# Convolution-kernel rows copied from tile to tile instead of through DRAM, and PSUM copies of the last block shared by two engines

## The chip, the core and the metric

One core of a Trainium2 chip runs the whole program. The metric is the device time of one launch in microseconds (us), from start to end of the program on that core. Five engines work beside each other, each through its own list of instructions in a fixed order: TensorE (PE in the profile; its weight loads are PEld), VectorE (DVE), ScalarE (ACT), GpSimd (POOL) and SyncE (SP). SP, ACT and POOL also issue DMA transfers; in the profile these issues are SPq, ACTq and POOLq.

## The reference

The reference computes one layer and all its gradients. With `x` of 2048 rows and 512 columns:

```
xn = layernorm(x)
K  = real(sum over n of C * exp(dt*A*l) * dt*B)      # 512 channels, l = 0..2047, 128 states
s  = irfft(rfft(xn, 4096) * rfft(K, 4096))[:2048] + xn * Dskip     # along the 2048 rows
g  = silu( silu(xn @ w1) @ w2 )                      # w1: 512 x 1792, w2: 1792 x 512
out = x + s * g
```

Its outputs are `out` and the gradients of `x`, of the seven arrays behind `K`, of `Dskip`, `w1` and `w2` for a given gradient of `out` (the gradient of an unused input is not among the work). Everything is bf16 outside; sums are made in fp32.

## The kernel before, in words

The 512 channels are worked in four blocks (b = 0 to 3) of 128. The long convolution is done as a Fourier transform written as matmuls. For each block in the forward part there are three generators, which the program weaves together:

- `gen_tables(b)` makes the convolution kernel K of the block. In two halves it builds powers of exp(dt*A) on DVE and ACT (`V`, `sn`, `E`, `YD`, `H`, lines 434 to 459), multiplies them into weight tiles `W` (line 468, DVE), and PE sums over the states into PSUM tiles `ps_k` (line 473), which ACT copies to `Xr`. At the end PE regroups `Xr` into two PSUM tiles `ps_e` (line 484), and ACT copies these in 12 pieces to the tile `KE` (lines 491 to 506). `KE` takes turns with `W` in one pool entry with two buffers (tag "W"). Its rows then go to the DRAM array `Kd` by four DMAs issued by ACT (line 508).
- `gen_conv_x(b)` transforms the block's columns of `xn`.
- `gen_conv_fwd(b)` loads `Kd` into the tile `Kb` by one DMA issued by SP (lines 531, 532), transforms it (`dft_fwd`, lines 289 to 318), multiplies by the transform of `xn` on DVE (`cplx_mul`, lines 341 to 355), transforms back (`dft_inv`, lines 321 to 338) and adds the skip term on DVE into `S_b` (lines 544, 545). `dft_fwd` and `dft_inv` hand 12 PSUM tiles of 128 x 1024 per call chain to an evacuation helper `ev`: four `dA` after line 299, four `dA` after line 315, four `dB` after line 328. In before, this helper is `k.evc`, which always uses ACT (line 45). The two transposed tiles `pt_f` between them always go to DVE (line 46). The PSUM tiles of the transforms come from a pool with two buffers ("pc"); those of the dense layers and transposes from one with three ("pf").

Beside these runs the dense forward part (`gen_ffn_fwd`): eight chunks of 256 rows, each with 56 matmuls at line 567 (PSUM to `hT` by ACT), two silu activations to `aT` at line 575, and 28 matmuls at line 585 (PSUM to `ob` or `YD` by ACT). When its last chunk is under way, `W1` is turned in place (seven PSUM tiles of transposes at line 112, copied back by ACT and DVE in turn). After block 3's tables, `gen_conv_fwd(3)`, the last chunk and two gate loops run together: line 613 (silu, ACT), 615 (DVE), 628 (derivative of silu, ACT), 629 and 631 (DVE). The first gate loop's silu and the second's derivative need different activation tables, so a change from one to the other costs an ACT_TABLE_LOAD. Then `last` columns are multiplied (line 1165, DVE), `W2` is turned, and the backward part begins, whose first dense matmuls are those at line 926.

The order of the Python text isn't the order on the engines. The framework plans each engine's list when the program is built, from its own estimates of when things will be ready, and within a pool entry it picks the buffer that its plan frees first. A change of a few lines therefore reorders instructions far around it. Each engine then works strictly in its planned order. Transfers issued by SP and ACT are counted on eight semaphores in turn; a transfer waits, before it is issued, for the last earlier one on its semaphore to land.

Of the kernel before, what the change touches and what calls it, by code (L numbers as in the profile page):

```python
# [13 lines left out]
BF16 = mybir.dt.bfloat16  # L14
# [4 lines left out]
P = 128  # L19
# [109 lines left out]
def run(gen):  # L129
    for _ in gen:  # L130
        pass
# [157 lines left out]
def dft_fwd(k, w8, U, ev):  # L289

    nc, pc = k.nc, k.pc
    A = w8.tile([P, 2, 16, P], BF16, name="dA", tag="w8")
    Av = A[:].rearrange("p c g k -> p (c g k)").rearrange("p (g c t e) -> p c g t e", c=2, t=16, e=4)
    B = w8.tile([P, 2, 16, P], BF16, name="dB", tag="w8")
    for c in range(2):
        for h in range(2):
            ps = pc.tile([P, 8, P], F32, name="ps_s1", tag="pc")
            for j in range(8):
                nc.tensor.matmul(out=ps[:, j], lhsT=k.TF[:, 8 * h + j, c, :], rhs=U(8 * h + j), start=True, stop=True)  # L299
            ev(Av[:, c, :, 8 * h:8 * h + 8, :], ps[:].rearrange("p t (g e) -> p g t e", e=4))  # L300
    yield
    for u in range(2):
        pt = pc.tile([P, 16, P], BF16, name="pt_f", tag="pc")
        for j in range(16):
            nc.tensor.transpose(out=pt[:, j], in_=A[:, u, j, :], identity=k.ident[:])
        k.evq(B[:, u], pt[:])
    for _ in range(LAG - 1):
        yield
    Bv = B[:].rearrange("p u (g h) k -> p u h g k", h=2)
    for u in range(2):  # L310
        for c in range(2):
            ps = pc.tile([P, 8, P], F32, name="ps_s2", tag="pc")
            for v in range(2):
                for h in range(2):
                    nc.tensor.matmul(out=ps[64 * h:64 * h + 64, 4 * v:4 * v + 4], lhsT=k.F2[:, c, :], rhs=Bv[:, u, h, 4 * v:4 * v + 4, :],  # L315
                                     start=True, stop=True)
            ev(A[:, c, 8 * u:8 * u + 8, :], ps[:])
    return A, B


def dft_inv(k, A2, Y, ev, consume):

    nc, pc = k.nc, k.pc
    for g0 in range(0, 16, 4):
        ps = pc.tile([P, 4, 32, 8], F32, name="ps_i2", tag="pc")
        for g in range(4):
            for c in range(2):
                nc.tensor.matmul(out=ps[:, g], lhsT=Y[:, c, g0 + g, :], rhs=k.I2[:, c].rearrange("p c m -> p (c m)"),  # L328
                                 start=(c == 0), stop=(c == 1))
        ev(A2[:].rearrange("p c t (g e) -> p g (c t) e", e=8)[:, g0:g0 + 4], ps[:])  # L330
    yield
    for h in range(2):
        ps = pc.tile([P, 8, P], F32, name="ps_i1", tag="pc")
        for j in range(8):
            t = 8 * h + j
            for c in range(2):
                nc.tensor.matmul(out=ps[:, j], lhsT=k.TI[:, 2 * t + c, :], rhs=A2[:, c, t, :], start=(c == 0), stop=(c == 1))
        consume(8 * h, 8, ps)


def cplx_mul(k, w8, a, b, conj=False):

    TT = k.nc.vector.tensor_tensor
    n = 8
    for g0 in range(0, 16, n):
        gs = slice(g0, g0 + n)
        t2 = w8.tile([P, 2, n, P], BF16, name="cm2", tag="cm2")
        TT(out=t2[:, 0], in0=b[:, 1, gs], in1=a[:, 1, gs], op=ALU.mult)
        TT(out=t2[:, 1], in0=b[:, 0, gs], in1=a[:, 1, gs], op=ALU.mult)
        TT(out=b[:, :, gs], in0=b[:, :, gs], in1=a[:, 0:1, gs].to_broadcast([P, 2, n, P]), op=ALU.mult)  # L350
        TT(out=b[:, 0, gs], in0=b[:, 0, gs], in1=t2[:, 0], op=ALU.add if conj else ALU.subtract)  # L351
        if conj:
            TT(out=b[:, 1, gs], in0=t2[:, 1], in1=b[:, 1, gs], op=ALU.subtract)
        else:
            TT(out=b[:, 1, gs], in0=b[:, 1, gs], in1=t2[:, 1], op=ALU.add)
# [61 lines left out]
def gen_tables(k, b):  # L417

    nc, tbl = k.nc, k.tbl
# [66 lines left out]
    KE = tbl.tile([P, 8, 8, 32], BF16, name="KE", tag="W", bufs=2)  # L486
    bc = lambda ap, n: ap.unsqueeze(2).to_broadcast([P, ap.shape[1], n, 32])
    ev = k.evk
# [15 lines left out]
    ev(KE[:, 2:8, 6:8, :], bc(B[:, 6:12], 2))  # L504
    ev(KE[:, 4:8, 5, :], B[:, 8:12])
    ev(KE[:, 4:8, 4, :], B[:, 12:16])
    for a in range(4):
        nc.scalar.dma_start(k.Kd[b, a].rearrange("i j r -> j i r"), KE[a:P:4].rearrange("p i t q -> p i (t q)"))
    yield


def spectrum_in(k, w8, b, which):
    t = w8.tile([P, 2, 16, P], BF16, name="sp_in", tag="w8")
    k.nc.sync.dma_start(t[:].rearrange("p c g k -> p (c g k)"), {"U": k.Ud, "K": k.KXd}[which][b])
    return t
# [11 lines left out]
def gen_conv_fwd(k, b):  # L527

    nc, dft = k.nc, k.dft
    bs = slice(b * P, b * P + P)  # L530
    Kb = dft.tile([P, 4, 16, 32], BF16, name="Kb", tag="t4")
    nc.sync.dma_start(Kb[:].rearrange("p a t q -> p a (t q)"), k.Kd[b].rearrange("a i (r s) x -> (i r) a (s x)", s=2))
    for _ in range(LAG):
        yield
    KX, A2 = yield from dft_fwd(k, dft, lambda t: Kb[:, :, t, :], k.evc)
    U = spectrum_in(k, dft, b, "U")
    nc.sync.dma_start(k.KXd[b], KX[:].rearrange("p c g k -> p (c g k)"))
    yield
    cplx_mul(k, dft, KX, U)
    S = dft.tile([P, 16, P], BF16, name="S_b", tag="t4")  # L540

    def consume(t0, n, ps):
        xd = dft.tile([P, 8, P], BF16, name="xd", tag="cm2")
        nc.vector.tensor_tensor(out=xd[:], in0=k.xn[:, t0:t0 + n, bs], in1=k.Dbc[:, bs].unsqueeze(1).to_broadcast([P, n, P]), op=ALU.mult)
        nc.vector.tensor_tensor(out=S[:, t0:t0 + n], in0=ps[:], in1=xd[:], op=ALU.add)
    yield from dft_inv(k, A2, U, k.evc, consume)
    k.S_b = S
    (nc.scalar if b == 3 else nc.sync).dma_start(k.Sd[b], S[:].rearrange("p t d -> p (t d)"))
    yield
# [496 lines left out]
def kernel(ctx, tc, A_u, A_A_re, A_A_im, A_B_re, A_B_im, A_C_re, A_C_im, A_log_dt, A_Dskip, B_x, B_w1, B_w2, grad_out,  # L1046
           out_0, out_1, out_2, out_3, out_4, out_5, out_6, out_7, out_8, out_9, out_10, out_11):
    nc = tc.nc
    k = KCtx()
# [10 lines left out]
    def pool(name, side=None, es=ctx, **kw):  # L1060
        kw.setdefault("bufs", 1)
        return es.enter_context(tc.tile_pool(name=name, side=side, reuse_waits="tile", **kw))
    dr = ctx.enter_context(tc.tile_pool(name="dram", bufs=1, space=DRAM))
    NB = 4
# [7 lines left out]
    k.dUd = dr.tile([NB, P, L], BF16, name="dUd")  # L1072
    k.Ud = dr.tile([NB, P, 4096], BF16, name="Ud")
    k.KXd = dr.tile([NB, P, 4096], BF16, name="KXd")
    k.Kd = dr.tile([NB, 4, 8, 32, 256], BF16, name="Kd")
    k.dKd = dr.tile([NB, 4, 8, 32, 256], BF16, name="dKd")
    k.Ed = dr.tile([NB, 2, P, 2 * 16 * NE * 4], BF16, name="Ed")
    k.Yd = dr.tile([NB, 2, P, 2 * 16 * P], BF16, name="Yd")
# [11 lines left out]
    es_f, es_x, es_t = (ctx.enter_context(ExitStack()) for _ in range(3))  # L1090
# [1 line left out]
    wt = pool("wt", es=es_d)  # L1092
    k.W1 = wt.tile([P, k.DK, F], BF16, name="W1")
    k.W2 = wt.tile([P, k.FT, D], BF16, name="W2")
    k.p1 = pool("p1", es=es_f)
    k.fp = pool("fp", es=es_f)
    with ExitStack() as es_s:
        wp = pool("setup", side="right", es=es_s)
        ldt = wp.tile([P, D], BF16, name="ldt")
        nc.scalar.dma_start(ldt[:], A_log_dt.unsqueeze(0).to_broadcast([P, D]))  # L1100
        nc.scalar.dma_start(k.Dbc[:], A_Dskip.unsqueeze(0).to_broadcast([P, D]))
        xl = load_x(k, wp)
        x_sb = next(xl)
        S = load_params(k, wp, 0, D, ("Ar", "Ai"))
        next(xl)
        nc.sync.dma_start(k.W1[:], B_w1.rearrange("(k p) f -> p k f", p=P))
        next(xl); next(xl)
        S.update(load_params(k, wp, 0, D, ("Br", "Bi", "Cr", "Ci")))
        nc.sync.dma_start(k.W2[:], B_w2.rearrange("(k p) d -> p k d", p=P))
        consts = make_consts(k, wp)  # L1110
        k.ident = k.const.tile([P, P], BF16, name="ident")
        nc.gpsimd.memset(k.ident[:], 0.0)
        nc.gpsimd.affine_select(out=k.ident[:], in_=k.ident[:], compare_op=ALU.not_equal, fill=1.0,
                                base=0, pattern=[[-1, P]], channel_multiplier=1)
        k.zero = k.const.tile([P, P], BF16, name="zero")
        nc.gpsimd.memset(k.zero[:], 0.0)
        k.onesf = k.const.tile([P, 1], F32, name="onesf")
        nc.gpsimd.memset(k.onesf[:], 1.0)
        k.ecst = k.const.tile([P, NE + len(Y_EXP)], F32, name="ecst")
        for i, e in enumerate(E_EXP + Y_EXP):  # L1120
            nc.gpsimd.memset(k.ecst[:, i:i + 1], float(e))
        ssm_magnitudes(k, wp, S, ldt[:])
        next(consts)
        ln = layer_norm(k, wp, x_sb)
        next(ln)
        k.XT = [turned_rows(k, k.fp, k.xn, c, "XT", k.evx) for c in range(2)]
        next(ln)
        next(consts)
        next(ln)
        ssm_weights(k, wp, S)  # L1130
        next(ln)
        run(consts)
# [83 lines left out]
```

## Time and profile before

| | |
|---|---|
| median of 3 runs | 691.67 us (687.14 to 695.03) |
| the profiled execution: its own time | 689.59 us |
| its span in the profile | 687.8 us |
| mean granted TensorE clock | 0.968 |
| PE busy | 594.7 us (86% of the span) |
| DVE busy | 505.9 us (74%) |
| ACT busy | 466.7 us (68%) |
| POOL busy | 81.7 us (12%) |
| `Kd` writes | 16 DMAs of 128 KB, issued by ACT |
| `Kb` loads | 4 DMAs of 512 KB, issued by SP |

Times in the text are microseconds from the start of the span. "Busy" counts compute instructions; the time in which ACT or SP issues a transfer is not in it. In a row of the timeline the first number is the start, the second the length, and in brackets stands how long the engine was idle before and what ended that. Some matmul records can be missing, and matmul ends are modelled.

### The profile page before, as it was taken

Reading aid. Unit: us, or ns where it says so; the run is one execution under the profiler, and the core shown is the slowest. Engines: PE = TensorE matmul, PEld = TensorE weight load, DVE = VectorE, ACT = ScalarE, POOL = GpSimd, SP = SyncE. Lnnn points to the kernel's source line nnn. Section 1 sums busy time; section 2 is a strip of 40 time slices with the busy share of each in tenths; the row PEclk is TensorE's granted clock in tenths of the full one; section 3 lists DMA queues with packets and bytes.
Section 4 is the critical chain, followed back from the end, with each engine's and each line's share of the span. In section 5 each row is a group of like instructions: output and inputs, shape, how many; then the busy total and the mean of one; then the engine's idle time right before and its main releaser. Section 6 shows DMA issues by size and latency. Waiting matters only on the chain. (4 is left out here: it accounts for less than half of the span.)

```text
span 687.8 us, 14419 instructions
## 1 busy us (share of the span) xinstructions
PE 594.7 (86%) x5884; PEld 434.3 (63%) x5884; DVE 505.9 (74%) x904; ACT 466.7 (68%) x628; POOL 81.7 (12%) x164
## 2 busy tenths in 40 slices
PE   0587987999999996689797999978998998999988
PEld 0455755676676664466575676747676765755877
DVE  6979998768968956979785969537688864756950
ACT  6878768889879888996656586335638764635531
POOL 2354100100101100000000000000002020123210
PEclk9988998999999999799999999999999999999999
DMA  9965455745746969777826755579979999238994
GB/s 286 341 152 210 179 202 193 274 165 215 278 138 239 325 234 314 240 252 242 274 77 217 219 187 192 150 175 219 258 151 287 209 221 229 89 115 273 228 285 103
DMA packets 158690, 148.54 MB, mean 216 GB/s; under 512 B 79264, under 2 KB 136096, under 8 KB 155040
## 3 DMA queue, kind: packets, MB, share of 16 engines
q1 hardware_dynamic: 145664, 125.07, 64.2%
q0 software_dynamic: 6064, 17.57, 6.8%
q10 hardware_dynamic: 6896, 4.98, 2.3%
q8 instruction: 46, 0.75, 0.5%
q14 instruction: 20, 0.16, 0.1%
HBM read 65.14 MB, written 64.10 MB: 188 GB/s over the span
## 5 line engine op out<-in xcount | busy, mean ns | idle before, releaser
L45 ACT CAST dA<-ps_s 128x1024 bf16<-128x1024 f32 x96 | 93.4, 1024 | 10.6 <-PE ps_s L299 6.8
L773 DVE TENSOR_TENSOR Tp<-Vb,Eb 128x1344 bf16<-128x1344 bf16 x64 | 51.8, 851 | 20.7 <-ACT Vb L45 11.8
L926 PE MATMUL ps_da<-doT,W 128*128 128x256 bf16 x448 | 60.9, 277 | 4.2 <-DVE dhT L928 2.6
L45 ACT CAST dB<-ps_i 128x1024 bf16<-128x1024 f32 x48 | 47.0, 1024 | 25.7 <-PE ps_i L328 18.9
L567 PE MATMUL ps_h<-XT,W 128*128 128x256 bf16 x448 | 63.0, 281 | 1.5 <-ACT hT L45 0.8
L928 DVE TENSOR_TENSOR dhT<-ps_da,dhT 128x512 bf16<-128x512 f32 x56 | 37.9, 686 | 35.5 <-PE ps_da L926 25.5
L328 PE MATMUL ps_i<-I,sp_in 128*128 128x256 bf16 x384 | 52.8, 286 | 8.9 <-DVE sp_in L351 6.4
L585 PE MATMUL ps_o<-W,aT 128*128 128x512 bf16 x224 | 55.2, 385 | 1.1 <-ACT aT L575 0.9
L937 PE MATMUL ps_dx<-W,dhT 128*128 128x512 bf16 x224 | 54.8, 379 | 0.4 <-DVE dhT L928 0.4
L567 PEld LDWEIGHTS <-W 128*128 128x128 bf16 x448 | 42.2, 100 | 16.3 <-issue 9.6
L328 PEld LDWEIGHTS <-sp_in 128*128 128x128 bf16 x384 | 37.5, 102 | 23.7 <-DVE sp_in L351 10.5
L926 PEld LDWEIGHTS <-W 128*128 128x128 bf16 x448 | 42.2, 99 | 15.8 <-issue 10.4
L969 PE MATMUL ps_w<-YD,a_tok 128*128 128x512 bf16 x224 | 51.5, 379 | 0.0
L987 PE MATMUL ps_w<-dh_tok,xn 128*128 128x256 bf16 x448 | 49.5, 272 | 2.3 <-DMA dh_tok<-DHd 2.3
L45 ACT CAST Vb<-ps_v 128x672 bf16<-128x672 f32 x64 | 42.3, 725 | 12.9 <-PE ps_v L763 12.9
L45 ACT CAST o<-ps_w 128x256 bf16<-128x256 f32 (+1 forms) x42 | 18.0, 439 | 48.5 <-PE ps_w L987 20.7
L987 PEld LDWEIGHTS <-xn 128*128 128x128 bf16 x448 | 43.6, 98 | 8.2 <-issue 3.0
L473 PE MATMUL ps_k<-W,YD 128*128 128x84 bf16 x512 | 29.7, 210 | 11.5 <-DVE W L468 6.7
L315 PE MATMUL ps_s<-dB,F 128*64 128x512 bf16 x192 | 32.5, 390 | 6.8 <-ACT dB L45 2.3
L473 PEld LDWEIGHTS <-YD 128*128 128x128 bf16 x512 | 25.4, 104 | 19.3 <-issue 13.8
L299 PEld LDWEIGHTS <-TF 128*128 128x128 bf16 x384 | 26.1, 101 | 18.0 <-issue 10.8
L585 PEld LDWEIGHTS <-aT 128*128 128x128 bf16 x224 | 21.1, 99 | 25.5 <-issue 3.9
(226 smaller groups left out, 1267.4 us busy)
## 6 DMA issues: line engine op xcount, KB each, us to landing
Yd<-YD SPq DMA_DIRECT2D x8, 1024.0 KB, 4.3
sp_in<-Ud SPq DMA_DIRECT2D x8, 1024.0 KB, 7.5
h_in<-Hd SPq DMA_DIRECT2D x14, 512.0 KB, 4.4
Ed<-E SPq DMA_DIRECT2D x8, 672.0 KB, 4.0
Eb<-Ed SPq DMA_DIRECT2D x8, 672.0 KB, 5.3
Hd<-hT POOLq DMA_DIRECT2D x8, 512.0 KB, 6.3
Ud<-dA SPq DMA_DIRECT2D x4, 1024.0 KB, 6.0
KXd<-dA SPq DMA_DIRECT2D x4, 1024.0 KB, 5.2
```

What stands on the lines that cost most here:

```text
L45: return self.nc.scalar.copy(out=out, in_=in_)
L315: nc.tensor.matmul(out=ps[64 * h:64 * h + 64, 4 * v:4 * v + 4], lhsT=k.F2[:, c, :], rhs=Bv[:, u, h, 4 * v:4 * v + 4, :], start=True, stop= ...
L328: nc.tensor.matmul(out=ps[:, g], lhsT=Y[:, c, g0 + g, :], rhs=k.I2[:, c].rearrange("p c m -> p (c m)"), start=(c == 0), stop=(c == 1))
L473: nc.tensor.matmul(out=ps[:, q], lhsT=Y[:, m % 2, q0 + 4 * u + q].rearrange("p j a -> p (j a)"), rhs=W[:, m, 4 * u + q].rearrange("p e a - ...
L567: nc.tensor.matmul(out=ps[:, j], lhsT=k.W1[:, dk, ft * P:ft * P + P], rhs=XTv[:, :, dk, :], start=(dk == 0), stop=(dk == DK - 1))
L585: nc.tensor.matmul(out=ps[:], lhsT=aT[:, ft, t * P:t * P + P], rhs=k.W2[:, ft, :], start=(ft == 0), stop=(ft == FT - 1))
L773: k.nc.vector.tensor_tensor(out=Tp[:, c, :, r ^ c].rearrange("p e (q w) a -> p q w e a", w=2), in0=Vb[:, :, c].rearrange("p q w (e a) -> p ...
L926: nc.tensor.matmul(out=ps[:, j], lhsT=k.W2[:, ft, dk * P:dk * P + P], rhs=dTv[:, :, dk, :], start=(dk == 0), stop=(dk == DK - 1))
L928: nc.vector.tensor_tensor(out=dh[:, i0:i0 + 2, :], in0=ps[:], in1=dh[:, i0:i0 + 2, :], op=ALU.mult)
L937: nc.tensor.matmul(out=ps[:], lhsT=dhs[ft // 8][:, ft % 8, t * P:t * P + P], rhs=k.W1[:, :, ft * P:ft * P + P], start=(ft == 0), stop=(ft ...
L969: nc.tensor.matmul(out=ps[:], lhsT=at[:, t, :], rhs=k.do[:, t, :], start=(t == 0), stop=(t == k.T - 1))
L987: nc.tensor.matmul(out=ps[:], lhsT=k.xn[:, t, dk * P:dk * P + P], rhs=dh[:, t].rearrange("p j n -> p (j n)"), start=(t == 0), stop=(t == k ...
```

## The change

`Kb` is now written directly from `KE`, by eight DMAs from tile to tile issued by SP (one for each group of 16 destination partitions) at the end of `gen_tables`; `Kd` in DRAM, its four writes and its load are gone. `Kb` has another order of its inner dimensions, and `dft_fwd` reads it accordingly; each DMA carries 128 rows of 512 bytes. `Kb` is allocated when the tables are made and handed on through `k.Kb`. For block 3 alone, the 12 PSUM copies of `gen_conv_fwd` go to ACT and DVE in turn. The pool `p1` (masks and small constants of the tables) is opened after `fp` and closed with the tables.

```
-    for a in range(4):
-        nc.scalar.dma_start(k.Kd[b, a].rearrange("i j r -> j i r"), KE[a:P:4].rearrange("p i t q -> p i (t q)"))
+    k.Kb[b] = k.dft.tile([P, 2, 4, 8, 32], BF16, name="Kb", tag="t4")
+    for i in range(8):
+        nc.sync.dma_start(k.Kb[b][16 * i:16 * i + 16].rearrange("r s a t q -> r (s a) (t q)"), KE[:, i].rearrange("p t q -> p (t q)"))
     yield
...
 def gen_conv_fwd(k, b):
     nc, dft = k.nc, k.dft
+    ev = Evac(nc, "AD") if b == 3 else k.evc
     bs = slice(b * P, b * P + P)
-    Kb = dft.tile([P, 4, 16, 32], BF16, name="Kb", tag="t4")
-    nc.sync.dma_start(Kb[:].rearrange("p a t q -> p a (t q)"), k.Kd[b].rearrange("a i (r s) x -> (i r) a (s x)", s=2))
+    Kb = k.Kb.pop(b)
     for _ in range(LAG):
         yield
-    KX, A2 = yield from dft_fwd(k, dft, lambda t: Kb[:, :, t, :], k.evc)
+    KX, A2 = yield from dft_fwd(k, dft, lambda t: Kb[:, t // 8, :, t % 8, :], ev)
...
-    yield from dft_inv(k, A2, U, k.evc, consume)
+    yield from dft_inv(k, A2, U, ev, consume)
...
-    k.Kd = dr.tile([NB, 4, 8, 32, 256], BF16, name="Kd")
+    k.Kb = {}
...
-    k.p1 = pool("p1", es=es_f)
     k.fp = pool("fp", es=es_f)
+    k.p1 = pool("p1", es=es_t)
```

## The prediction, made before the changed kernel had run

> **What bounds the kernel now.** I read the page's busy table first (PE 86%, no engine full), then a table of stages. The two programs list the same matmuls, and from the 2425th on (the first at line 926) all engines' orders agree, so the time of that matmul decides. It starts at 298.48. The stages are cut at the end of block 0's `KE` copies, at the first matmul on `Kb`, at the end of block 3's regrouping, and there. Columns: stretch, its length, then busy time of PE, PEld, DVE, ACT, POOL, granted clock, DMA share, GB/s.
>
> ```profile
> 99.18:111.66 12.48, 6.25 (x77) 4.92 (x78) 9.27 (x17) 6.63 (x9) 0.57 (x1) 0.73 0.58 197
> 111.66:245.50 133.84, 130.70 (x1390) 91.70 (x1389) 109.70 (x152) 117.75 (x170) 10.87 (x14) 1.00 0.65 235
> 245.50:298.48 52.98, 37.43 (x379) 27.84 (x377) 37.68 (x54) 47.99 (x52) 0.00 (x0) 0.85 0.78 250
> 298.48:687.80 389.32, 354.20 (x3463) 264.00 (x3461) 264.39 (x506) 218.48 (x292) 37.77 (x68) 0.99 0.78 203
> ```
>
> The long second stage is PE's (98%). In the third ACT is fullest (48.0 of 53.0) and PE waits. The first is a hole: PE is busy for half of it, at a clock of 0.73. The timeline says why:
>
> ```profile
> 99.18 4.78 ACTq L508 DMA_DIRECT2D Kd<-KE  x4
> ...
> 104.00 0.44 ACT L45 CAST Xr<-ps_k 128x336 bf16<-128x336 f32 x1 [4.36 <-issue]
> ...
> 104.50 0.97 PE L473 MATMUL ps_k<-W,YD 128*128 128x84 bf16 x16 [2.94 <-ACT Xr L45]
> ...
> 107.31 1.63 DVE L468 TENSOR_TENSOR W<-E,CT 128x1344 bf16<-128x1344 bf16 x2 [3.12 <-DMA Kd<-KE]
> ...
> 108.22 0.32 PE L473 MATMUL ps_k<-W,YD 128*128 128x84 bf16 x2 [2.76 <-DVE W L468]
> ```
>
> ACT issues the four `Kd` writes for 4.78 us and meanwhile copies nothing, so PE waits 2.94 for a PSUM copy; then `W` waits 3.12 for those writes, because it gets `KE`'s buffer, and PE another 2.76.
>
> **Part 1, the DRAM passage.** Removed: 16 writes and 4 loads. The writes hold ACT for 4.78, 2.60, 3.39 and 2.58 us after the four blocks. The loads cost 0.37 us of SP each and no matmul on `Kb` waits for a DMA, so the shorter way itself is worth 0; worth something is ACT's time and the buffer.
>
> Added: 32 SP transfers of 64 KB. Price of an issue: SP rows 0.32 to 0.37, the `Kd` rows on ACT 0.58 to 0.63; I take 0.35, as the issuer is SP, so 2.8 for eight (bounds 2.6 and 5.0). Landing: 2.2 (`Kd<-KE`, 128 KB) to 3.8 (`Kb<-Kd`, 512 KB), once 6.6. So `Kb` is there 5.0 to 11.6 us after `KE`. Queued behind the eighth on SP are `Yd` and `Sd` writes, and the table load `mag` behind the first. In block 0 that `mag` slips from 94.1 to 99.6, lands 5.2 later at 104.8, and its reader comes at 106.6: covered. In block 3 `Kb` is read 13 us after `KE` (below): covered; at the upper bound too. Without that cover each us late is a us on the end.
>
> The Trainium skill speaks against this part ("DMA: Bandwidth & Descriptors", Rules for kernel authors): coalesce transfers, since under 64 KB one pays mostly overhead. This change cuts one load into eight of just that size. In the trace a 64 KB store to DRAM (`out_dram<-o`, SP) lands in 1.5 us, so size isn't the cost here; were eight to run one behind the other, it would be 12 us, just within block 3's cover.
>
> Now the first hole in the changed order, walked by the rows' durations. ACT, free at 99.15 (end of the `KE` copies): two `ob` and two `hT` copies (0.60 each) to 101.5, `Xr` to 101.9 and, after PE's 0.7, another to 103.1. DVE: the planner now lets the second `W` take the buffer that PE frees instead of `KE`'s; its wait is for PE (102.6), its start 103.65 after three table operations. PE has 19 dense matmuls and 8 transposes more laid between, 2.7 us of cover. By 107.4 PE has done what it had at 111.9 before, and 23 dense matmuls and 8 transposes beyond. But then line 585 needs `aT`, and ACT reaches that after `sn`, `hT`, `Xr`, `sn`, `Xr` only at 110.9: PE idles some 2.5 at 109. From there on ACT is busy without a break (8 `dA` from 114.2 to 122.2, against 112.4 to 119.9). Carried on, block 1's regrouping ends at 135.7 instead of 132.7, with 16 matmuls of line 567 (2.78/24 = 0.116 each) and 25 of line 585 (6.21/28 = 0.222) done beyond: 7.4 − 3.0 = **4.4 us gained**. The stage after has only 3.1 us of PE idle time before, so ACT's further 6 us of freed issue time there save little; I take 0, bounds −2 (the new order has its own stalls) and +3. Gain by the end of stage two: 4.4, bounds 1.5 to 7.5 (all idle time of stage one, 6.2, and 1.5 of slow clock).
>
> **Part 2, the shared copies.** Six of block 3's 12 copies leave ACT: 6 × 1.02 = 6.1 us. They come to DVE. No row of before has DVE copying fp32 from PSUM; neighbours of the size are 0.68 (bf16 PSUM to `XT`) and 1.22 (adding fp32 PSUM, line 545). I take 1.22, the row with the same source type: 7.3 us; 4.1 at the other end. The Trainium skill ("VectorE: DVE Perf Modes", Why PSUM operands drop a tier) gives fp32 from PSUM the plain rate, the same choice.
>
> ```profile
> L45 ACT CAST dA<-ps_s 128x1024 bf16<-128x1024 f32 x96 | 93.4, 1024 | 10.6 <-PE ps_s L299 6.8 <-PE ps_s L315 3.6
> ...
> L545 DVE TENSOR_TENSOR S_b<-ps_i,xd 128x1024 bf16<-128x1024 f32 x8 | 9.8, 1220 | 14.4 <-PE ps_i L337 14.4
> ...
> L46 DVE COPY XT<-pt_t 128x1024 bf16<-128x1024 bf16 x8 | 5.4, 681 | 1.8 <-PE pt_t L112 1.8
> ```
>
> By totals stage three would gain: ACT 48.0 − 6.1 + 2.6 (the new order switches tables four times instead of two, two loads of 1.28 more) = 44.5, DVE 37.7 + 7.3 = 45.0, against 53. But the order decides. Call the start of the last 28 matmuls of line 585 T (before: 251.45).
>
> - Before, these 6.2 us cover gate work: ACT runs three silu from T+0.8, DVE three `ds` products and a skip sum. In the changed order ACT's two copies of those matmuls' results stand ahead of the silus, and DVE's next is a `W2` transpose that PE makes after them. So from T to T+6.8 both mostly idle.
> - Then the first copies do go faster: the `pt_f` transposes start at T+11.4 (before T+13.5), their copies end at T+15.9 (before T+17.1).
> - From T+6.8 on DVE has 39 us of work without a gap up to the first product of line 1165: six copies (7.3), two `pt_f` copies (2.4), all eight products of each of lines 615, 629, 631 (15.3), two halves of complex products (7.9), skip terms (3.8), three `W2` copies (2.0). With 0.9 of small waits and the product itself (0.7) that ends at T+47.3. Before, T+39.4.
> - Behind it on PE: transposes of `YD`, 8 matmuls of line 299, then 32 transposes, whose last `dA` copy on ACT ends at T+49.2; line 926 starts at T+50.3, against T+47.0. That is 3.3 later.
>
> T itself: the turning of `W1` now stands between the last inverse transform and line 585, its copies on DVE behind two `S_b` sums; by the same walk T comes 0.15 later relative to the end of stage two. **Tail: +3.5 us**, bounds −1 (copies at 0.68 on DVE and small waits gone) and +8 (half-speed matmuls, since PE idles more: the chain holds some 11 us of them; before, the clock there was 0.85).
>
> **Rest.** `p1`'s place and closing hold nothing that the tail waits for: 0. After 298.48 the orders agree; I shift that stage rigidly (bounds ±1).
>
> **Sum.** −4.4 + 3.5 = −0.9 on 689.59, so 688.7. The median shown lies 2.1 above the profiled execution, so I say **690.8** for it.
>
> **Rivals.**
> 1. *The tail is not longer.* ACT was its fullest engine, and totals of 45 in place of 53 speak for it: with −1 in the tail and 4.4 to 7.5 ahead of it the sum is −5.4 to −8.5, some 684.5. Against it: the 6 us in which both engines stand behind line 585.
> 2. *Slower: DVE becomes the bound of the last block.* If T's idle stretch is as walked and the slow clock takes the chain through lines 315, 328, 337 and 299, the tail is +8 and more; it decides as soon as stage one gives less than that. With a gain of 1.5 (ACT's unbroken queue up to 122 holds PE) the sum is +6.5 to +9, about 699. For it: DVE has no gap after T+6.8 in the walk.
> 3. *It doesn't do what it says*: the eight transfers run one by one behind their semaphores and the queue blocks. Then `Kb` lands 12 us or more after `KE`, with up to +3 in block 3 and late `Yd`, `mag` elsewhere: about +2 to +5 on the sum, 694. Against: 2.2 us landings of the like.
>
> **Numbers.** Forecast (within 1%, the bound of what a measurement of this kernel can tell, as its runs spread by 1.1%): 0.47. Rival 1: 0.25, of which 0.18 beyond 1%. Rival 2: 0.23, of which 0.21 beyond. Rival 3: 0.05, within. So faster 0.18, same 0.61, slower 0.21. Range 682 to 700: rival 1's far end nearly, and rival 2's.
>
> **What would show it.** Right: no idle of 2.9 and 2.8 on PE near 104 and 108; a wait of line 585 for `aT` near 109; block 1's regrouping ending near 136; ACT and DVE idle beside the last matmuls of line 585, then DVE full for some 40 us; DVE copies of 1.2 us; the first matmul of line 926 within 2 us of 298. Wrong: DVE copies near 0.7, a `Kb` wait on PE, or a second stage whose PE idle time grows beyond 5 us.

## The result, and the profile after

| | before | after |
|---|---|---|
| median | 690.90 us | 687.57 us |
| ratio after / before, 95% interval | | 0.9937, 0.9916 to 0.9959 |
| the profiled execution: its own time | 689.59 us | 689.14 us |
| its span | 687.8 us | 687.4 us |
| PE, DVE, ACT busy | 594.7, 505.9, 466.7 us | 594.4, 512.3, 464.8 us |
| start of the last 28 matmuls of line 585 (586 after) | 251.45 | 246.47 |
| first matmul of line 926 (927 after) | 298.58 (298.48 by its weight load, where the stages were cut) | 296.40 |

By the ratio the changed kernel is faster by 0.6%, that is 4.4 us, with an interval of 2.8 to 5.8. Its forecast was 690.8 and "within 1%". The ratios leave out slow executions, those over 1.5% above the fastest of their kernel, which the medians here, 3.3 us apart, include, and the profile of the kernel with the sharing alone, further down, is of a slow one. A line added in the change shifts later line numbers by one: line 586 of after is line 585 of before, and so on.

The stages first, cut at the times used for before (the same columns: stretch, length, busy time of PE, PEld, DVE, ACT, POOL, clock, DMA share, GB/s):

```profile
99.18:111.66 12.48, 10.08 (x127) 7.96 (x127) 11.84 (x21) 11.25 (x17) 1.46 (x2) 1.00 0.67 237
111.66:245.50 133.84, 128.52 (x1405) 90.85 (x1404) 111.19 (x153) 117.10 (x169) 9.99 (x13) 0.99 0.62 218
245.50:298.48 52.98, 35.95 (x325) 25.54 (x324) 41.84 (x59) 45.13 (x44) 0.00 (x0) 0.77 0.80 259
298.48:687.80 389.32, 353.55 (x3447) 263.77 (x3443) 262.63 (x504) 215.47 (x290) 37.78 (x68) 0.99 0.78 200
```

The hole of the first stage is closed: PE works 10.08 of its 12.48 us (6.25 before) at full clock (0.73 before). In the third PE has less left to do (35.95 us in place of 37.43) and does it at a lower clock, 0.77 in place of 0.85. The timeline of after shows the first hand-over:

```profile
98.28 4.97 SPq L509 DMA_DIRECT2D Kb<-KE  x7
...
103.59 1.61 DVE L468 TENSOR_TENSOR W<-E,CT 128x1344 bf16<-128x1344 bf16 x2
...
104.49 0.25 PE L473 MATMUL ps_k<-W,YD 128*128 128x84 bf16 x2 [0.28 <-DVE W L468]
...
108.37 1.95 ACT L576 ACTIVATE aT<-hT 128x2048 bf16<-128x2048 bf16 x1
...
110.18 1.59 ACT L45 CAST hT<-ps_h 128x512 bf16<-128x512 f32 x3
...
110.85 1.02 PE L586 MATMUL ps_o<-W,aT 128*128 128x512 bf16 x4 [2.03 <-ACT hT L45]
```

SP issues the copies, ACT goes on with its own work, `W` starts at 103.59 without a wait, and PE's two waits of 2.94 and 2.76 us are gone. What is late next is `aT`: PE waits 2.03 us for ACT at 110.85. Then the last block, also from the timeline of after:

```profile
237.94 7.62 SPq L509 DMA_DIRECT2D Kb<-KE  x8
...
246.47 6.21 PE L586 MATMUL ps_o<-W,aT 128*128 128x512 bf16 x28
...
249.74 0.59 ACT L45 CAST YD<-ps_o 128x512 bf16<-128x512 f32 x1 [2.05 <-PE ps_o L586]
252.71 0.59 ACT L45 CAST YD<-ps_o 128x512 bf16<-128x512 f32 x1 [2.39 <-PE ps_o L586]
253.16 0.69 DVE L46 COPY W<-pt_t 128x1024 bf16<-128x1024 bf16 x1 [6.57 <-PE pt_t L112]
253.20 1.06 ACT L614 ACTIVATE g<-YD 128x1024 bf16<-128x1024 bf16 x1
...
254.50 1.22 DVE L46 CAST dA<-ps_s 128x1024 bf16<-128x1024 f32 x1 [0.65 <-PE ps_s L299]
...
257.79 1.95 PE L305 MATMUL pt_f<-ident,dA 128*128 128x128 bf16 x32 [0.81 <-DVE dA L46]
```

While PE runs the last 28 matmuls of line 586, ACT stands for 2.05 and 2.39 us and DVE for 6.57; the first silu (`g`, line 614) comes at 253.20, 6.7 us after these matmuls began. Before, ACT ran three silus from 0.8 us after that point:

```profile
251.45 6.21 PE L585 MATMUL ps_o<-W,aT 128*128 128x512 bf16 x28
...
252.22 2.98 ACT L613 ACTIVATE g<-YD 128x1024 bf16<-128x1024 bf16 x3
```

On the chip nothing that the trace shows holds the first silu of after for so long: the last load of `YD` that was issued before it landed at 240.6, and the last copy out of `KE` at 247.3. It waits in ACT's list, where the plan put it behind the two copies.

The groups of after, with shapes kept apart, answer to the three price rows:

```profile
L45 ACT CAST dA<-ps_s 128x1024 bf16<-128x1024 f32 x92 | 90.2, 1027 | 14.9 <-PE ps_s L299 12.4
L546 DVE TENSOR_TENSOR S_b<-ps_i,xd 128x1024 bf16<-128x1024 f32 x8 | 9.8, 1222 | 8.5 <-PE ps_i L337 8.4
L46 DVE COPY XT<-pt_t 128x1024 bf16<-128x1024 bf16 x8 | 5.4, 682 | 1.8 <-PE pt_t L112 1.8
L46 DVE CAST dA<-ps_s 128x1024 bf16<-128x1024 f32 x4 | 4.9, 1219 | 0.7 <-PE ps_s L299 0.6
```

The last row is new: a copy of 128 x 1024 fp32 from PSUM by DVE takes 1.219 us, the price of the `S_b` row and not that of `XT`. The Trainium skill ("VectorE: DVE Perf Modes", Why PSUM operands drop a tier) says that fp32 from PSUM goes at DVE's plain rate; this row agrees.

### The profile page after: what moved, and what is told of

It reads as the page before. It is cut to its first block, busy times and chain, and to the rows that moved or that the text cites. A ratio compares the mean times of both kernels' runs of the same rounds, so it can differ in the third digit from the quotient of the medians.

```text
span 687.4 us, 14472 instructions
## 1 busy us (share of the span) xinstructions
PE 594.4 (86%) x5884; PEld 434.1 (63%) x5884; DVE 512.3 (75%) x910; ACT 464.8 (68%) x624; POOL 81.7 (12%) x164
## 4 chain that ended last, share of the span: by engine, by line
issue 73%; DVE 8%; PE 5%; POOL 5%; DMA 5%; ACT 2%; SPq 0%; POOLq 0%; ACTq 0%; DVEq 0%
PE ps_w L988 3%; DMA dh_tok<-DHd 3%; POOL Hd L577 1%; POOL out_dram L844 1%; PE ps_o L586 1%; DVE st L270 1%; DMA out_dram<-gout 1%; DVE jk L1021 1%; POOL out_dram L973 1%; ACT dA L45 1%; DVE o L1031 1%; DMA out_dram<-o 1%; DMA x_sb<-in_A_u_dram 1%; POOL out_dram L659 1%; DVE E L447 1%
## 5 line engine op out<-in xcount | busy, mean ns | idle before, releaser
L45 ACT CAST dA<-ps_s 128x1024 bf16<-128x1024 f32 x92 | 90.2, 1027 | 14.9 <-PE ps_s L299 12.4
L568 PE MATMUL ps_h<-XT,W 128*128 128x256 bf16 x448 | 61.2, 280 | 1.4 <-ACT hT L45 0.6
L586 PE MATMUL ps_o<-W,aT 128*128 128x512 bf16 x224 | 58.1, 392 | 4.0 <-ACT hT L45 2.0
L45 ACT CAST dB<-ps_i 128x1024 bf16<-128x1024 f32 x46 | 45.1, 1038 | 19.4 <-PE ps_i L328 19.1
L988 PE MATMUL ps_w<-dh_tok,xn 128*128 128x256 bf16 x448 | 51.1, 278 | 4.6 <-DMA dh_tok<-DHd 4.5
L927 PEld LDWEIGHTS <-W 128*128 128x128 bf16 x448 | 42.4, 99 | 15.9 <-issue 10.3
L46 DVE COPY dB<-pt_f 128x2048 bf16<-128x2048 bf16 x24 | 28.5, 1218 | 14.6 <-PE pt_f L305 14.5
L315 PE MATMUL ps_s<-dB,F 128*64 128x512 bf16 x192 | 29.7, 388 | 8.2 <-ACT dA L45 3.2
L970 PEld LDWEIGHTS <-a_tok 128*128 128x128 bf16 x224 | 21.1, 98 | 22.7 <-issue 0.7
```

The source lines that it names most:

```text
L45: return self.nc.scalar.copy(out=out, in_=in_)
L46: return self.nc.vector.tensor_copy(out=out, in_=in_)
L568: nc.tensor.matmul(out=ps[:, j], lhsT=k.W1[:, dk, ft * P:ft * P + P], rhs=XTv[:, :, dk, :], start=(dk == 0), stop=(dk == DK - 1))
L586: nc.tensor.matmul(out=ps[:], lhsT=aT[:, ft, t * P:t * P + P], rhs=k.W2[:, ft, :], start=(ft == 0), stop=(ft == FT - 1))
L927: nc.tensor.matmul(out=ps[:, j], lhsT=k.W2[:, ft, dk * P:dk * P + P], rhs=dTv[:, :, dk, :], start=(dk == 0), stop=(dk == DK - 1))
L970: nc.tensor.matmul(out=ps[:], lhsT=at[:, t, :], rhs=k.do[:, t, :], start=(t == 0), stop=(t == k.T - 1))
```

## The experiments

### How they are read

A kernel's executions differ by some 1% from one to the next, and one profile can't settle 4 us: from the 3700th matmul on PE's order is the same in before, after and every experiment, and yet their profiled executions took from 232 to 240 us for that part. Between two chips the ratio may shift too: one kernel below gave 0.9852 on one and 0.9896 on the other, with intervals that overlap. On the first of these chips were measured that 0.9852, the two kernels with block 3 by DRAM and the one with SP and POOL, shared; on the other all the rest but after, whose chip is not on record. So times are told by ratio and interval, and places in the trace only up to the last block. There I use two marks: T, the start of the last 28 matmuls of the second dense layer (line 585), and the 2552nd weight load on PE (counted from 0), which in before and after is that of the first matmul of line 937 (938). Every matmul has one weight load and the records of these are complete, so that the n-th can be counted in any order of work. The times of weight loads in this and the later texts are shifted, by up to 0.3 us, so that each kernel's first one starts at 18.36 as in before. The third column of times is the stretch from the 2000th to the 2552nd, the last block with what leads into it, for the same number of matmuls, though not always for the same ones. Two profiles of one kernel differ in it by 1.1 us (the DRAM way with writes by SP) and 0.4 (the same, shared), so less than about 1 us there says nothing.

| kernel | T | 2552nd | 2000th to 2552nd | ratio to before, interval |
|---|---|---|---|---|
| before | 251.45 | 312.0 | 71.9 | |
| after | 246.47 | 309.5 | 74.2 | 0.9937, 0.9916 to 0.9959 |
| DRAM way, writes by SP | 244.37 | 308.6 | 73.8 | 0.9932, 0.9890 to 0.9975 |
| the same again | 243.51 | 308.7 | 74.9 | 0.9951, 0.9918 to 0.9985 |
| after, copies by ACT | 266.12 | 330.4 | 79.6 | 1.0219, 1.0164 to 1.0275 |
| direct copies only | 246.06 | 312.3 | 77.3 | 1.0047, 1.0006 to 1.0088 |
| shared PSUM copies only | 252.13 | 312.5 | 71.5 | 0.9982, 0.9940 to 1.0023 |
| direct, block 3 by DRAM | 245.30 | 309.1 | 74.9 | 0.9895, 0.9846 to 0.9945 |
| the same, shared | 245.48 | 310.9 | 76.5 | 0.9883, 0.9833 to 0.9934 |
| direct by SP and POOL, shared | 243.64 | 306.2 | 73.3 | 0.9867, 0.9818 to 0.9916 |
| the same, not shared | 243.40 | 305.9 | 72.9 | 0.9949, 0.9917 to 0.9982 |
| DRAM way by SP, shared | 243.49 | 308.0 | 74.4 | 0.9852, 0.9794 to 0.9909 |
| the same again | 244.29 | 309.4 | 74.8 | 0.9896, 0.9862 to 0.9931 |
| after, `p1` as before | 245.90 | 308.4 | 73.9 | 0.9924, 0.9893 to 0.9954 |

"Shared" means that block 3's 12 PSUM copies go to ACT and DVE in turn.

### Is it the way through DRAM, or who issues it?

The edit of before, in one place:

```
     for a in range(4):
-        nc.scalar.dma_start(k.Kd[b, a].rearrange("i j r -> j i r"), KE[a:P:4].rearrange("p i t q -> p i (t q)"))
+        nc.sync.dma_start(k.Kd[b, a].rearrange("i j r -> j i r"), KE[a:P:4].rearrange("p i t q -> p i (t q)"))
```

> This kernel is before with one word changed: the four writes to DRAM of each block are issued by SP instead of ACT. The passage through DRAM, its 512 KB load and KE's buffers stay. Theory (ACT's time at the issue was the cost, the way through DRAM is not): no 2.9 us wait for Xr near 104, PE busy 9 to 11 of the 12.5 us in 99 to 112, the last 28 matmuls of line 585 at 246 to 248, ratio 0.992 to 0.996, that is no slower than the changed kernel. Rival (the shorter way, or the 4 MB of DRAM traffic saved, is the gain): those matmuls stay at 250 to 252 and the ratio at 0.998 to 1.002. In between, with W still waiting some 3 us for KE's buffer near 107: 0.996 to 0.998, and then the buffer has a share of its own.

It measured 0.9932, as fast as the changed kernel, with the DRAM passage whole. T, at 244.37, came earlier than the 246 to 248 expected. Its first stage, in the same columns as above:

```profile
99.18:111.66 12.48, 10.09 (x126) 7.99 (x128) 11.84 (x20) 11.24 (x16) 1.46 (x2) 1.00 0.82 279
```

and its timeline there:

```profile
98.88 1.17 ACT L45 CAST ob<-ps_o 128x512 bf16<-128x512 f32 x2
...
99.10 4.00 SPq L508 DMA_DIRECT2D Kd<-KE  x4
...
103.46 1.62 DVE L468 TENSOR_TENSOR W<-E,CT 128x1344 bf16<-128x1344 bf16 x2
...
104.37 0.25 PE L473 MATMUL ps_k<-W,YD 128*128 128x84 bf16 x2 [0.28 <-DVE W L468]
...
110.72 1.33 PE L585 MATMUL ps_o<-W,aT 128*128 128x512 bf16 x4 [2.03 <-ACT hT L45]
```

These are the rows of after, 0.13 us earlier, down to the wait of 2.03 for `hT`. The four writes take 4.00 us of SP, where nobody waits. And `W` doesn't wait for `KE`'s buffer, although `KE` is read by the same writes as before, the last of which lands only at 105.25: with ACT free, the plan gives `W` the other buffer. So neither gain needs the direct copies. Moving the issues off ACT brings both, ACT's time and the free buffer; no kernel here has one without the other, so their shares aren't known.

The DRAM way isn't quite free at the end, however. In block 3 its `Kb` lands 7.2 us after T, and the first matmuls on it wait, which those of before and after don't:

```profile
251.63 1.05 PE L299 MATMUL ps_s<-Kb,TF 128*128 128x128 bf16 x16 [0.66 <-DMA Kb<-Kd]
```

The opposite edit, in the changed kernel:

```
     for i in range(8):
-        nc.sync.dma_start(k.Kb[b][16 * i:16 * i + 16].rearrange("r s a t q -> r (s a) (t q)"), KE[:, i].rearrange("p t q -> p (t q)"))
+        nc.scalar.dma_start(k.Kb[b][16 * i:16 * i + 16].rearrange("r s a t q -> r (s a) (t q)"), KE[:, i].rearrange("p t q -> p (t q)"))
```

> This kernel is the changed one, except that its 32 direct copies are issued by ACT instead of SP. By ACT's own rows (0.58 to 0.63 us an issue) eight take 4.6 to 5 us after each block. Theory (ACT's time at the issue was the cost): the hole comes back, with a wait of PE of 2 to 4 us for a PSUM copy near 104, the last 28 matmuls of line 586 at 249 to 252, and with the changed kernel's longer tail the ratio is 0.999 to 1.006. Rival (the shorter way is the gain, whoever issues it): those matmuls at 246 to 248, ratio 0.993 to 0.996.

```profile
98.80 5.53 ACTq L509 DMA_DIRECT2D Kb<-KE  x6
...
104.36 0.44 ACT L45 CAST Xr<-ps_k 128x336 bf16<-128x336 f32 x1 [5.33 <-DMA Kb<-KE]
...
104.85 1.28 PE L473 MATMUL ps_k<-W,YD 128*128 128x84 bf16 x16 [3.41 <-ACT Xr L45]
...
107.20 1.63 DVE L468 TENSOR_TENSOR W<-E,CT 128x1344 bf16<-128x1344 bf16 x2 [3.12 <-DMA Kb<-KE]
```

This timeline has the hole of before again, with direct copies: 3.41 us on PE behind `Xr`, 3.12 on DVE behind the buffer. The direction was as expected, the size was not: T came at 266.12, expected at 249 to 252. It measured 1.0219, some 15 us, because the loss grows with the later hand-overs: against before, the 700th weight load is 0.4 us late, the 1000th 5.6, the 1500th 8.3 and the 2000th 10.7. PE waits 2.8 us at line 328 after the second hand-over (138.0), and 2.6 at line 337 after the fourth (262.8), for `dB` copies that stand behind ACT's issues. I had priced the first hole and taken it for all.

### Each part alone

Direct copies and the moved pool, without the sharing:

```
-    ev = Evac(nc, "AD") if b == 3 else k.evc
+    ev = k.evc
```

> This kernel has the direct copies and the moved pool, but block 3's twelve copies all stay on ACT, as before the change. Theory (ACT's issue time and the freed buffer are the gain, the shared copies only lengthen the tail): the hole at 99 to 112 is gone as in the changed kernel (PE busy about 10 of its 12.5 us), the last 28 matmuls of line 586 start at 246 to 247, and the last block takes the 47 us it took before rather than 50, so 2 to 3 us less than the changed kernel: 683 to 686, ratio to before 0.989 to 0.993. The order of the tail is planned anew, though, with all four dA copies and one more table load on ACT ahead: if that order is the worse one, the ratio is 0.994 to 0.998. Rival (the shared copies are the gain, as they relieve ACT in its fullest stage): 0.999 to 1.003.

It measured 1.0047: slower than before, and 1.1% slower than the changed kernel. T came as expected, the rest did not. Neither account holds: the hand-over is a gain (T is 5.4 us earlier than before), but all of it is lost by the 2552nd weight load (312.3 against 312.0), and sharing wins a part back (309.5). The timeline says where:

```profile
244.54 0.60 SPq L509 DMA_DIRECT2D Kb<-KE  x1
...
246.06 6.21 PE L586 MATMUL ps_o<-W,aT 128*128 128x512 bf16 x27
...
249.32 0.58 ACT L45 CAST YD<-ps_o 128x512 bf16<-128x512 f32 x1 [2.05 <-PE ps_o L586]
252.30 0.58 ACT L45 CAST YD<-ps_o 128x512 bf16<-128x512 f32 x1 [2.39 <-PE ps_o L586]
252.78 1.06 ACT L614 ACTIVATE g<-YD 128x1024 bf16<-128x1024 bf16 x1
253.74 3.75 ACT L45 CAST dA<-ps_s 128x1024 bf16<-128x1024 f32 x4
253.87 5.86 SPq L615 DMA_DIRECT2D Gd<-g  x3
257.34 2.04 ACT L614 ACTIVATE g<-YD 128x1024 bf16<-128x1024 bf16 x2
...
259.82 0.75 SPq L515 DMA_DIRECT2D sp_in<-Ud  x1
...
266.05 0.69 DVE L348 TENSOR_TENSOR cm<-sp_in,dA 128x1024 bf16<-128x1024 bf16 x1 [3.42 <-DMA sp_in<-Ud]
```

ACT idles beside line 586 exactly as in after, and from 252.3 on it has the silus and the copies at once: it is busy without a break to 285. The third silu ends at 259.4. SP holds its store (`Gd`) in order, so the load of `sp_in` behind it is issued only at 259.82, and DVE's complex product waits 3.42 us for it. Before issued that load later still, 14.3 us after T as against 13.8, and its product waited 0.6 for it; so the late load alone doesn't explain the loss.

The sharing alone, on the DRAM passage of before:

```
+    ev = Evac(nc, "AD") if b == 3 else k.evc
```

The two calls that follow take `ev` in place of `k.evc`.

> This kernel keeps the DRAM passage of before, and only block 3's twelve copies go to ACT and DVE in turn. Theory (nothing is gained by sharing): the hole at 99 to 112 stays (PE busy some 6 of 12.5 us, clock near 0.73), the last 28 matmuls of the second dense layer start at 251 to 252 as before, and from there the tail takes 46 to 50 us against 47.1: ratio 0.999 to 1.005. Rival (the shared copies are the gain): a tail of 43 us or less, ratio 0.993 to 0.995.

```profile
252.13 2.11 PE L586 MATMUL ps_o<-W,aT 128*128 128x512 bf16 x8
...
252.90 2.98 ACT L614 ACTIVATE g<-YD 128x1024 bf16<-128x1024 bf16 x3
...
299.15 0.49 PE L927 MATMUL ps_da<-doT,W 128*128 128x256 bf16 x3
```

Here the hole stays (PE busy for 6.08 us of the first stage), T is 252.13, and the silus keep their early place. The first matmul of line 927 comes 47.0 us after T, as against 47.1. At 0.9982 the interval holds no change as well as a gain of 0.6%.

So in the old order the sharing doesn't lengthen the tail, and it doesn't move the silus: the kernel with direct copies only has them late without it, this one has them early with it. What moved them should be block 3's hand-over.

### Block 3's hand-over

By the code, the gate tiles get memory that the tables held until these are closed (`es_t`, on the same side of the memory), and `KE` is one of the tables. `KE` is held until its last copy has landed. The last of the eight is issued at 244.54 in the kernel with direct copies only. The next kernel sends block 3 alone through DRAM again, in four writes by SP:

```
+    if b < 3:
...
+    else:
+        for a in range(4):
+            nc.sync.dma_start(k.Kd[b, a].rearrange("i j r -> j i r"), KE[a:P:4].rearrange("p i t q -> p i (t q)"))
```

Under `b < 3` stand the direct copies as they are in after; for b = 3 the load of `Kb` is that of before.

> Blocks 0 to 2 use the direct copies, block 3 alone goes through DRAM again, its four writes issued by SP; all of block 3's PSUM copies are on ACT. Against the kernel with direct copies only, one thing differs: block 3's hand-over. Theory formed on that kernel's trace (the eight direct copies of block 3 take SP 7.6 us and keep the tables' memory, which the gate tiles get next, until some 248; so the first gate loop's silus are planned behind the copies of line 586 and ACT is short by 5 us later): here the silus run beside the last 28 matmuls of line 586, these start at 246 to 247, the 2552nd weight load comes at 306.5 to 309 in place of 312.3, ratio 0.991 to 0.997 in place of 1.0047. Rival (the direct layout, the moved pool or the further table loads cost it): 2552nd weight load at 311 to 313, ratio 1.001 to 1.006.

It measured 0.9895 where the kernel with direct copies only has 1.0047 (on the other chip; the 1.5% between them is more than the shift between chips seen above). Its timeline:

```profile
245.28 0.38 SPq L542 DMA_DIRECT2D Kb<-Kd  x1
245.30 6.21 PE L596 MATMUL ps_o<-W,aT 128*128 128x512 bf16 x27
...
248.57 0.58 ACT L45 CAST YD<-ps_o 128x512 bf16<-128x512 f32 x1 [2.05 <-PE ps_o L596]
249.05 2.95 ACT L624 ACTIVATE g<-YD 128x1024 bf16<-128x1024 bf16 x3
...
251.90 0.57 ACT L45 CAST YD<-ps_o 128x512 bf16<-128x512 f32 x1
...
253.98 0.60 SPq L519 DMA_DIRECT2D sp_in<-Ud  x1
```

All three silus now stand ahead of the second copy, `sp_in` is issued 8.7 us after T in place of 13.8, DVE waits for no `sp_in`, and up to 283 ACT loads three tables in place of five (1.28 us each). One correction to my own expectation: SP's "7.6 us" for the eight copies is partly a wait. In after, the first is issued at 237.9, the second only at 241.2, when ACT has written what it reads; from there on seven go in 4.4 us. The four writes of this kernel take 2.62.

T, at 245.30, and the 2552nd weight load, at 309.1, lie just outside the ranges expected; the ratio is better than expected. Up to that load the trace shows 3.2 us of the gain, a third of what the ratios say. Whether it is SP's time or the held memory that moves the silus in the plan, no kernel here tells apart: both end earlier together.

The same kernel with sharing:

> The one before it with block 3's copies shared by ACT and DVE again. Theory (sharing only pays back what the late silus take from ACT, and does little where they are early, 0.998 alone in the old order): 0.988 to 0.995, within 0.4% of the kernel without sharing. Rival (sharing is worth 7 us in itself, as between the kernel with direct copies only and the changed one): 0.981 to 0.986.

0.9883 against 0.9895: with the silus early, sharing gains nothing that shows in the ratio, as expected. The stretch from the 2000th to the 2552nd weight load, 76.5 us, is longer than that of after (74.2), though, with the silus early. So late silus aren't the only thing that can lengthen the tail.

### Splitting the issues instead

```
     for i in range(8):
-        nc.sync.dma_start(k.Kb[b][16 * i:16 * i + 16].rearrange("r s a t q -> r (s a) (t q)"), KE[:, i].rearrange("p t q -> p (t q)"))
+        (nc.sync, nc.gpsimd)[i % 2].dma_start(k.Kb[b][16 * i:16 * i + 16].rearrange("r s a t q -> r (s a) (t q)"), KE[:, i].rearrange("p t q -> p (t q)"))
```

> The changed kernel with its direct copies issued by SP and POOL in turn. POOL's issues of like transfers take 0.56 to 0.90 us and POOL is idle beside them. Theory (the eight issues on one queue hold the tables' memory and SP's later loads too long): the fourth pair is issued within 4 us, the silus come ahead of the second copy of line 586, 2552nd weight load at 306 to 308.5 in place of 309.5, ratio 0.987 to 0.993. Rival (POOL's transfers land later and hold the first transform of block 3, which would show as a wait of line 299 for Kb): ratio 0.996 to 1.003.

0.9867. The view of the tile `Kb` (instructions, count, nanoseconds min/median/max, first and last start) for this kernel

```profile
L509 SPq DMA_DIRECT2D Kb<-KE x16: 547/562/746, 94.8 to 240.0; - x16
L509 POOL DMA_DIRECT2D Kb<-KE x16: 528/532/552, 98.1 to 240.1; - x16
```

and for after:

```profile
L509 SPq DMA_DIRECT2D Kb<-KE x32: 547/589/1963, 95.2 to 245.0; - x32
```

The last transfer of block 3 is issued at 240.1 instead of 245.0, the silus run beside line 586, and no matmul waits for `Kb`. The fourth pair is issued 4.9 to 5.0 us after the first copy, not within 4; the 2552nd weight load, at 306.2, is in the range expected. The first matmul of line 927 comes 47.8 us after T, in place of 49.9 in after, with the same 300 matmuls between. It is the changed kernel with half of the issues on another engine, and its interval ends where that of the changed kernel begins; as it ran on the other chip, the size of its gain is uncertain by the shift told above. The Trainium skill ("DMA: Bandwidth & Descriptors", Rules for kernel authors) says that spreading DMAs over engines brings no bandwidth and saves only issue time. The trace agrees: the transfers don't land sooner (3.8 and 3.5 us here, 2.9 in after). Here the issue time was the thing to save.

The same without sharing:

> Direct copies in all blocks, issued by SP and POOL in turn; block 3's PSUM copies all on ACT. It is to the kernel with SP and POOL sharing the issues (0.9867) what the kernel with direct copies only (1.0047) is to the changed one (0.9937). Theory (sharing the PSUM copies only pays back what late silus cost; with the issues split the silus run beside line 586): last 28 matmuls of line 586 at 243 to 245, 2552nd weight load at 305 to 308, ratio 0.983 to 0.992, so within 0.5% of 0.9867. Rival (with direct copies, sharing is worth some 7 us in any order): 0.994 to 1.000.

T, at 243.40, was as expected and so was the 2552nd weight load (305.9, the earliest of all), but the ratio was 0.9949, not within 0.5% of 0.9867 and inside the rival's range. By the trace sharing is worth nothing here up to the 2552nd weight load (306.2 with it); by the times it is worth up to 0.8%, in executions on two chips. The first matmul of line 927 comes 45.0 us after T here (303 matmuls between) and 47.8 with sharing (300): up to that mark sharing costs time.

### Is sharing worth something where the silus are early?

The DRAM way with SP's writes, with sharing, alone and once more beside its partner on one chip:

> The DRAM passage with its writes issued by SP (0.9932 of before on its own), and block 3's copies shared by ACT and DVE. Theory (the two parts add up where the silus are early): 0.9932 times 0.998, so 0.988 to 0.995, not slower than the changed kernel. Rival (sharing is worth 7 us in itself): 0.980 to 0.985.

> The DRAM passage with its writes issued by SP, a second time, to stand beside the next one on the same chip. Theory: 0.988 to 0.995.

> The same with block 3's PSUM copies shared, a second time. Theory (sharing is worth little where the silus are early): within 0.4% of the one before it. Rival (it is worth the 0.8% that lay between the two when they ran apart, 0.9932 and 0.9852): 0.6 to 1.0% below it.

They measured 0.9852, then 0.9951 without and 0.9896 with sharing. The difference of 0.55% on one chip lies between the two expectations, and the two intervals overlap; by the medians of all executions, 687.13 and 685.06 us, it is 0.3%. Of the four pairs with early silus the differences are 0.2% (before), 0.1% (block 3 by DRAM), 0.55% (DRAM way by SP) and 0.8% (SP and POOL), all one way; the traces show none of it up to the 2552nd weight load. So sharing is worth something between 0 and 0.8% there, behind the last block if anywhere, and this stays open.

### The pool

```
+    k.p1 = pool("p1", es=es_f)
     k.fp = pool("fp", es=es_f)
-    k.p1 = pool("p1", es=es_t)
```

> The changed kernel with the pool p1 opened ahead of fp and closed late, as it was before the change. Theory (the pool's place is worth nothing): like the changed kernel, 0.991 to 0.997. Rival (closing p1 early frees room that the last block's tiles need): 0.998 or more.

0.9924 against 0.9937: no difference. All engines' orders are the same in both.

## Why the prediction was right, and where it was not

**The hole: right.** PE's two waits went, `W` started at 103.59 (walked: 103.65), and the wait for `aT` and `hT` came at 109 to 110.9 with 2.03 us (walked: 2.5 at 109). Block 1's regrouping ended at 134.46, not 135.7. T came 4.98 us earlier; the walk gave 4.4 less 0.15.

**The reason for it: right on one half.** The gain is the issues' leaving ACT, as the DRAM kernel with SP's writes shows: 0.9932 and 0.9951 against 0.9937. With equal sharing the direct way issued by SP even has the higher ratio (1.0047 against 0.9932 and 0.9951 without; with sharing 0.9937 against 0.9852 and 0.9896, where the intervals of the first and the last overlap). "The shorter way itself is worth 0" holds but for the wait of line 299, 0.7 to 1.0 us, that the DRAM kernels with SP's writes have in block 3. But the buffer, which I named beside ACT's time, needs no direct copy: that kernel has the way and the buffers of before, and its `W` starts without a wait.

**The price of an issue on SP: mis-sized.** I took 0.35 us; the row says 0.589 in the median and 1.963 at most. Eight take 4.7 us, near the upper bound of 5.0. The rows of 0.32 to 0.37 that I went by were the short ones: the median of before's 293 SP issues is 0.43, the longest 5.66. The price goes with the transfer, and I had put it down to the issuer: four `Kd` writes cost SP 2.56 us after block 1, where they had cost ACT 2.60. What in a transfer sets it, no run here shows. So the Trainium skill's rule to coalesce ("DMA: Bandwidth & Descriptors", Rules for kernel authors), which I weighed and set aside, was nearer than I took it for: the transfers land quickly (2.9 us in the median), but their issues add up. The covers that I named held: no matmul waited on a DMA for `Kb`, and landing took 2.4 to 6.7 us against 2.2 to 6.6. What I did not name was the gate work of block 3, which comes behind the copies on SP and gets memory that they read.

**The tail: the sum right, partly by luck, and the cause of the order wrong.** From T to the first matmul of line 927 it took 49.9 us against 47.1, +2.8 where I said +3.3 (and +3.5 with T's 0.15). DVE's copies cost 1.22 as taken, the `pt_f` transposes started at T+11.3 (walked: T+11.4), their copies ended at T+15.2 (T+15.9), the first product of line 1166 at T+44.7 (T+47.3). From there to line 927 it took 5.2 us and not the 3.0 of the walk; that the end agrees is luck, as two errors of over 2 us cancel. And I wrote all of it down to part 2, as if the shared copies brought the changed order. The walk used that order as a given and never asked which edit made it. Sharing alone leaves the tail at 47.0; the direct copies alone make the stretch to the 2552nd weight load 5.4 us longer; sharing takes 3.1 of these back. In this order the sharing is worth 1.1%, the difference between 1.0047 and 0.9937. How the 2.8 us of after divide stays open. With the issues split over SP and POOL and the silus early, 2.1 of them go (47.8). But the kernels that send block 3 through DRAM by SP and share take 51.6 to 52.2 us for the same 300 matmuls, also with early silus. And the two kernels with early silus and no sharing whose hand-over was shortened in block 3 alone or split over SP and POOL reach line 927 after 44.9 and 45.0 us (304 and 303 matmuls): there the sharing does lengthen the stretch to this mark, though hardly that to the 2552nd weight load.

**The rest of stage two: taken as 0, +0.7 by T.** PE's idle time there grew from 3.1 to 5.3 us all the same, which I had named as a mark of being wrong at 5. The largest piece is a new wait of 1.1 us of line 586 for `aT`; the mark was a poor one, as the hand-over had brought more than the walk gave it.

**The sum.** −0.9 was forecast for the first matmul of line 927 and −2.2 came. The 2.1 us that I added to get from the profiled execution to the median came from three executions; over twenty it was 1.3 in before and −1.6 in after. The kernel's times say −4.4. The remaining 2 us can't be placed: in the two profiles shown the part behind that matmul is 1.8 us longer in after, and profiles of that part vary by more, as told above.

**The rivals.** The first (no longer tail) failed by its own mark, +2.8. The second (DVE becomes the bound) didn't come about either: DVE was busy for 29.7 of the 32.5 us from 252.5 to 285, close to the walk, but in the kernel with the sharing alone, where the first product of line 1166 comes 3.1 us later after T than in before, line 927 still starts no later. The third (transfers one by one) failed by the landings.

## What to carry to other kernels

Before a data path is shortened, look at who issues its transfers: here one word, the issuing engine, was worth all that the direct copy won, and the direct copy issued by the busy engine cost 2.2%. When a walk through a changed order finds a stall, ask which edit put the order there, by building each part alone, since the part that looks like the cause may be the one that pays for it. And count what a long hand-over does to the work that is planned behind it, on the queue that issues it and in the memory that it holds, also when its reader has time. The kernels here with a shorter one and shared copies (0.9852 and 0.9896 for DRAM writes by SP, 0.9867 for copies split over SP and POOL, 0.9883 for block 3 by DRAM) lie 0.4 to 0.9% ahead of the changed kernel, though most of them ran on the chip with the lower ratios.

## What the runs showed that I had not expected

An issue of a tile-to-tile copy of 128 rows of 512 bytes took SP 0.55 to 0.60 us, at most 1.96, while the shortest of SP's issues in before took 0.32 (median 0.43); POOL issued the same copies in 0.53.

The kernel with direct copies only and the DRAM kernel with SP's writes have the same PE order from the 2257th matmul on, and lie 1% apart. What differs behind that point is the place of the gate work on ACT and DVE and of the stores and loads that hang on it on SP; from 292 on all engines' orders agree. From the 2300th to the 2552nd weight load the first takes 35.5 us and the second 34.3 and 35.1, from there to the 3700th 142.7 against 136.0 and 137.3. In this last stretch the granted clock was 0.940 in the first and 0.975 in both profiles of the second. But after and the kernel with `p1` as before, whose orders are the same throughout, also differ in it by 3.9 us (139.4 and 135.5), so the traces don't show how much of the 1% belongs there, or why.
